# A linear-attention and expert-routing kernel: routing maximum, states' terms, first weights and last outputs rearranged

## The chip, the cores and the metric

The kernel runs on one core of one Trainium2 chip. The metric is the device time of one execution in microseconds (us), as the median of several runs. One execution was also taken by the hardware profiler, which records every instruction of the engines: PE (TensorE matmul; its weight loads are listed as PEld), DVE (VectorE), ACT (ScalarE), POOL (GpSimd) and SP (SyncE, which here only issues transfers).

## The reference

Two blocks follow one another. The first is a linear attention with a decaying state, for 4 batches, 8 heads, 768 steps and 48 elements a head. The second sends each token to one of 8 experts; a local gate decides whether a token takes its own choice or that of the token before it.

```python
for t in range(S):                                   # attention, per batch and head
    cur = einsum('bhd,bhe->bhde', u[None] * kt, vt)
    y[:, :, t] = einsum('bhd,bhde->bhe', rt, state + cur)
    state = w[None, :, :, None] * state + einsum('bhd,bhe->bhde', kt, vt)

logits = einsum('bsd,de->bse', x, w_gate)            # experts; x is y with heads joined, D = 384
local_gate = 1 / (1 + exp(-einsum('bsd,de->bse', x, w_local)))
for b, s:
    fresh_e = argmax(logits[b, s])
    e = fresh_e if s == 0 or local_gate[b, s] < 0.5 else prev_e
    p = softmax(logits[b, s])
    out[b, s] = p[e] * (maximum(x[b, s] @ w1[e], 0) @ w2[e])      # F = 1024
```

## The kernel before

The attention works on 16 items, one for each batch and pair of heads (`M = 16`; item n is batch n // 4, pair n % 4). Sequences are cut into 6 chunks of 128 steps. `Attention.run` is a loop over steps n = 0 to 16 whose order of calls is the order in which each engine gets its instructions; nothing is reordered afterwards. In a step, PE works for item n - 1 and prepares item n + 1:

- `load(n)` issues an item's transfers on SP's queue (`rk`, `kv`, `vT`), three items ahead.
- `scale(n)` on POOL makes `rw` (L229), `ke` (L212) and `pd` (L216), two instructions each. `keys(n)` on DVE makes `kw` (L236) with a factor that lies in PSUM.
- `added(n)` (L248) forms on PE the terms that the chunks add to the state, in the tile `T`, and `states(n)` (L254) runs the decay over them with a DVE scan. `T` is a slice of the one-bank PSUM tile `mp`, which the router also uses.
- `scores(n, g)` (L283) forms the scores within chunks on PE in one of the two `pairs` of PSUM banks, taken in turn by `banks`. The mask is applied on DVE (`am`, L285).
- `own(n)` starts the output `y` on PE (L264), and DVE multiplies it by the values (L268). `inside(n)` (L292) adds the scores' part. `before(n)` (L305) adds the state's part and copies `y` to `xT` (L309, on ACT; for the last item one head on ACT and one on DVE).
- `turn(n)` (L318) transposes an item's outputs to token order in a pair of banks, ACT copies them to `x` (L320), and after a batch's last item they go to DRAM (L323). `logits(b)` (L331) and `token_logits(b)` (L337, L338) compute a batch's routing logits.

Waits follow the tiles: an engine that writes a PSUM bank waits for those that still read that bank of the same tile.

The router works in groups of two batches. For the first group its work is spread over steps 9 to 16 (`g = 8` in `run`): `experts_of` in step 9 (maximum L672, comparison L673, product L674, then L676 to L678 at the end of the step), `keys` (L685) and `runs` in step 10, `turn_runs` (L695), `last` (L702) and `one_hot` (L709 to L713) in step 11, `counts` (L722, L723) and `ranks` (L729 to L738) in step 12, `slots` (L774 to L777) and `columns` (L782) in step 13, `numbers` (L787) in step 14, `places` (L793, `ohq`) in steps 13 and 14, `summed` (L800), `copied` (L806) and `head` (L810 to L831) in step 15. `head` yields the token numbers with which POOL gathers the first expert's rows (L1047, into `xg`).

`Experts` follows: two first units whose experts are fixed, then eight blocks. `fetch` issues a unit's two weight matrices (1.5 MB each). Unit 0's are issued on SP in step 14 of the loop, behind the item loads; SP itself waits for nothing else there, so that they go out at 83.4 and 84.1 us, in step 12 of PE's time. `hidden` (L1074) and `output` (L1161) are an expert's two products; the rows are transposed first (L1060). PE's order at the border is: last `inside` and `before`, the last batch's `logits`, the transposes of the gathered rows, `token_logits`, `hidden`. The PSUM banks of the attention's pools are handed on to the experts' pools in the order in which they lie.

Of the kernel before, what the change touches and what calls it, by code (L numbers as in the profile page):

```python
# [11 lines left out]
F32 = mybir.dt.float32  # L12
# [49 lines left out]
class Attention:  # L62
# [13 lines left out]
    def __init__(self, tc, st, rk_d, kv_d, vT_d, x_d, w_t, wp_d, kept, ident, lt, mp):  # L76
# [13 lines left out]
        self.two = pool("two", 2)  # L90
        self.four = pool("four", 4)
        ps = pool("ps", 1, space=PSUM)

        self.pairs = [ps.tile([P, 2, 512], F32, name=f"pair{i}") for i in range(2)]
        self.py = pool("py", 1, space=PSUM)

# [160 lines left out]
    def own(self, n):  # L257

        nc, t = self.nc, self.items[n]
        t["y"] = y = self.py.tile([P, 2, 512], F32, name="y")  # L260
        for p in range(2):
            for h in range(2):
                q = slice(h * DP, h * DP + DH)
                nc.tensor.matmul(y[p * DP:(p + 1) * DP, h, :C2 * P].rearrange("p (c t) -> p c t", c=C2),  # L264
                                 lhsT=self.w_t[q, t["hp"], 1:2].to_broadcast([DH, DP]),
                                 rhs=t["pd"][q].rearrange("p (c k) t -> p k c t", k=2)[:, p],
                                 start=True, stop=True)
        nc.vector.tensor_mul(y[:, :, :C2 * P], y[:, :, :C2 * P], t["vT"].rearrange("p h c t -> p h (c t)"))  # L268

# [17 lines left out]
    def inside(self, n):  # L287
        nc, t = self.nc, self.items[n]
        for c2, h in [(c2, h) for c2 in range(C2) for h in range(2)]:
            for p in range(2):  # L290
                c = 2 * c2 + p
                nc.tensor.matmul(t["y"][p * DP:(p + 1) * DP, h, c2 * P:(c2 + 1) * P],  # L292
                                 lhsT=t["v"][:, (2 * c + h) * DH:(2 * c + h) * DH + DP],
                                 rhs=t["am"][:, c // 3, h, c % 3], start=False, stop=False, skip_group_check=True)

    def before(self, n):
        nc, t = self.nc, self.items[n]
        if t["hp"] == 0:
            self.xTs[t["b"]] = self.late.tile([P, H, C2 * P], F32, name="xT")
            self.xs[t["b"]] = self.late.tile([P, NCH, D], F32, name="x", bufs=2)  # L300
        for c in range(1, NCH):
            p, c2 = c % 2, c // 2
            for h in range(2):
                q = slice(h * DP, h * DP + DH)
                nc.tensor.matmul(t["y"][p * DP:p * DP + DH, h, c2 * P:(c2 + 1) * P],  # L305
                                 lhsT=t["S"][q, :, c - 1], rhs=t["rw"][q, c],
                                 start=False, stop=True, skip_group_check=True)
        for h in range(2) if n == B * HP - 1 else (slice(0, 2),):
            (nc.vector.tensor_copy if h == 1 else nc.scalar.copy)(  # L309
                self.xTs[t["b"]][:, 2 * t["hp"]:2 * t["hp"] + 2][:, h], t["y"][:, h, :C2 * P])  # L310

    def turn(self, n, banks):

        nc, b, h0 = self.nc, self.items[n]["b"], 2 * self.items[n]["hp"]
        xT, x = self.xTs[b], self.xs[b]
        for h in range(2):
            for c2 in range(C2):
                nc.tensor.transpose(banks[h][:, c2 * P:c2 * P + U], xT[:U, h0 + h, c2 * P:(c2 + 1) * P], self.ident[:U, :U])  # L318
        for h in range(2):
            nc.scalar.copy(x[:, :, (h0 + h) * DH:(h0 + h + 1) * DH],  # L320
                           banks[h][:, :C2 * P].rearrange("p (c e) -> p c e", e=DP)[..., :DH])
        if h0 == H - 2:
            nc.scalar.dma_start(out=self.x_d[b * S:(b + 1) * S, :].rearrange("(c p) d -> p c d", p=P), in_=x)  # L323

    def logits(self, b, bank):

        nc, xT = self.nc, self.xTs[b]
        self.lTs[b] = lT = self.late.tile([P, C2 * P], F32, name="lT")
        for h in range(H):
            j = h % 4  # L330
            nc.tensor.matmul(bank[32 * j:32 * j + 32, :C2 * P], lhsT=self.wp[:, h], rhs=xT[:, h], start=(h < 4), stop=(h >= 4))  # L331
        nc.scalar.copy(lT, bank[:, :C2 * P])
# [8 lines left out]
    def run(self, router, fetch, heads):  # L341
# [11 lines left out]
        for n in range(M + 1):  # L353
            if n + AHEAD - 1 < M:
                self.load(n + AHEAD - 1)
            elif n + 2 == M:
                fetch()
            if n == 0:
# [32 lines left out]
            if n < M:  # L391
                self.turn(n - 2, pair("tp"))
                if n == 3:
                    self.reciprocals(3)
                if n < 5:
                    self.keys(n)
                if n > 3:
                    if n != g + 3:
                        self.added(n)
                    self.states(n)  # L400
# [6 lines left out]
            if n == g + 5:  # L407
                router.slots(0)
                router.columns(0)
            if n == g + 6:  # L410
                router.numbers(0)
            if n == M:
                router.shares(0)
            if n + 1 < M:
                self.scale(n + 1)
            if 3 <= n < 6:
                router.constants(n - 3)
            if n == M:
                self.turn(M - 2, pair("tp"))
            self.inside(n - 1)  # L420
            if n == g + 3:

                router.turn_runs(0, mp[:, mp_end:])
            self.before(n - 1)
            if n == 6:
                router.cast()
# [5 lines left out]
            if n == g + 7:  # L432

                router.summed(0, 0)
                router.copied(0, self.nc.vector.tensor_copy)
                router.head(pair("tb")[0])
                heads()
# [8 lines left out]
            if n % HP == 0:  # L446
# [4 lines left out]
                if n == 4:  # L451
                    self.scores(5, 0)()
                    self.scores(5, 1)()
                    self.keys(6)
                if n == g + 4:
                    router.counts(0, [mp, mp[:, E * NC // 2:]])
                    router.ranks(0, (0,))
# [104 lines left out]
class Router:  # L562
# [103 lines left out]
    def experts_of(self, i, parts=(0, 1)):  # L666
# [3 lines left out]
        if 0 in parts:  # L670
            nc.vector.memset(lt[:, g["z"]].rearrange("p (b c) e -> p b c e", c=NCH)[0:1, :, 0, E:], -1.0)
            nc.vector.tensor_reduce(g["mx"], lg, axis=AX.X, op=Alu.max)  # L672
            nc.vector.tensor_tensor(g["eq"], lg, spread(g["mx"], 2, E), op=Alu.is_equal)  # L673
            nc.vector.tensor_tensor(g["eq"], g["eq"], spread(self.down, 1, g["nc"]), op=Alu.mult)  # L674
# [108 lines left out]

    def numbers(self, i):

        g = self.g[i]
        self.nc.vector.tensor_tensor(g["val"], g["eqv"], spread(self.t1[:, g["z"]], 2, E * ST), op=Alu.mult)  # L787

# [186 lines left out]
class Experts:  # L975
# [49 lines left out]
    def fetch(self, i, engine):  # L1025
# [9 lines left out]
        u["w2"] = wp.tile([P, FK, D], F32, name="w2t", tag="w2t")  # L1035
        engine.dma_start(out=u["w2"].rearrange("p m f -> p (m f)"), in_=w2)

    def gather(self, i, tiles=None, after=None):
# [534 lines left out]
def kernel(  # L1573
# [41 lines left out]
    with ExitStack() as st, tc.manual_schedule():  # L1615
# [4 lines left out]
        att = Attention(tc, st, rk_d, kv_d, vT_d, x_d, w_t, wp_d, kept, ident, lt, router.mp)  # L1620
        att.run(router, lambda: ex.fetch(0, nc.sync), lambda: ex.gather(0))
        ex.open(st)
# [93 lines left out]
```

## Time and profile before

| what | us |
|---|---|
| median of 3 runs (range) | 383.04 (382.22 to 383.92) |
| the profiled execution's own time | 383.35 |
| its span, first to last instruction | 381.6 |
| PE busy | 366.2 |
| DVE busy | 251.4 |
| POOL busy | 150.7 |
| ACT busy | 107.2 |

Steps of the attention loop, by the start of their transposes (L318): step 9 at 62.97 us, 10 at 69.63, 11 at 75.56, 12 at 81.84, 13 at 89.03, 14 at 96.20, 15 at 101.88, 16 at 107.69. The experts' first product (L1074) starts at 114.67.

A line of the timeline gives the start, the length, the engine, the line of the code, the operation, output and inputs by tile name, their shapes, a count of merged instructions, and in brackets the engine's idle time before it with what ended that time. Matmul ends are modelled, so that a busy PE is not PE at its peak; a releaser is inferred, and of several awaited semaphores it is the one that came last. Fp32 products show as two PE instructions each.

### The profile page before, as it was taken

Reading aid. Unit: us, or ns where it says so; the run is one execution under the profiler, and the core shown is the slowest. Engines: PE = TensorE matmul, PEld = TensorE weight load, DVE = VectorE, ACT = ScalarE, POOL = GpSimd, SP = SyncE. Lnnn points to the kernel's source line nnn. Section 1 sums busy time; section 2 is a strip of 40 time slices with the busy share of each in tenths; the row PEclk is TensorE's granted clock in tenths of the full one; section 3 lists DMA queues with packets and bytes.
Section 4 is the critical chain, followed back from the end, with each engine's and each line's share of the span. In section 5 each row is a group of like instructions: output and inputs, shape, how many; then the busy total and the mean of one; then the engine's idle time right before and its main releaser. Section 6 shows DMA issues by size and latency. Waiting matters only on the chain. (4 is left out here: it accounts for less than half of the span.)

```text
span 381.6 us, 9675 instructions
## 1 busy us (share of the span) xinstructions
PE 366.2 (96%) x3846; PEld 322.8 (85%) x3846; DVE 251.4 (66%) x720; ACT 107.2 (28%) x290; POOL 150.7 (39%) x212
## 2 busy tenths in 40 slices
PE   7999999998999999999999999999999999999992
PEld 6776777776759998999999999999998899899971
DVE  6888778978934646596557857758758758466400
ACT  4132232232222211322323233243234233232210
POOL 8689999887222043311422313222323123012022
PEclk9999999999999999999999999999999999999997
DMA  7999999989116881820661254145246156064011
GB/s 252 410 411 408 408 401 326 364 308 381 60 33 226 315 344 37 315 94 23 215 207 55 53 207 189 49 173 214 69 166 227 39 179 228 12 219 165 3 37 36
DMA packets 17477, 74.97 MB, mean 196 GB/s; under 512 B 2729, under 2 KB 6586, under 8 KB 14864
## 3 DMA queue, kind: packets, MB, share of 16 engines
q1 hardware_dynamic: 10048, 56.89, 39.8%
q0 software_dynamic: 3424, 9.52, 7.6%
q10 hardware_dynamic: 3952, 7.87, 5.7%
q8 instruction: 32, 0.52, 0.5%
q14 instruction: 21, 0.17, 0.1%
HBM read 64.83 MB, written 9.51 MB: 195 GB/s over the span
## 5 line engine op out<-in xcount | busy, mean ns | idle before, releaser
L1273 POOL DMA_INDIRECT out_dram<-yo,sid x27 | 26.7, 988 | 102.4 <-ACT yo L1268 75.0
L1124 PE MATMUL h<-exT,w1t 128*128 128x168 f32 (+4 forms) x240 | 54.9, 327 | 0.0
L1128 DVE TENSOR_TENSOR hT<-h,hs 128x168 f32<-128x168 f32 (+3 forms) x60 | 21.1, 351 | 46.5 <-PE h L1124 30.4
L1047 POOL DMA_INDIRECT xg<-x_d,gid x29 | 31.2, 1076 | 37.3 <-DVE sm L882 17.4
L1124 PEld LDWEIGHTS h<-exT,w1t 128*128 128x128 f32 x240 | 41.6, 190 | 0.3 <-issue 0.3
L1074 PE MATMUL h<-exT,w1t 128*128 128x192 f32 (+1 forms) x192 | 38.3, 338 | 0.0
L1193 PE MATMUL y<-factors,sums 128*128 128x192 f32 x168 | 36.8, 326 | 0.0
L1124 PE MATMUL h<-xs,ws 128*128 128x168 f32 (+4 forms) x144 | 35.2, 326 | 0.0
L216 POOL TENSOR_TENSOR pd<-rk 128x384 f32<-128x384 f32 x32 | 31.4, 1002 | 8.6 <-PE y L264 6.2
L285 DVE TENSOR_TENSOR am<-pair,kept 128x768 f32<-128x768 f32 x32 | 30.0, 952 | 6.2 <-PE pair L283 5.5
L1074 PEld LDWEIGHTS h<-exT,w1t 128*128 128x128 f32 x192 | 32.3, 190 | 1.5 <-issue 0.2
L1124 PEld LDWEIGHTS h<-xs,ws 128*128 128x128 f32 x144 | 25.5, 190 | 4.3 <-ACT hs L1131 1.2
L1193 PEld LDWEIGHTS y<-factors,sums 128*128 128x128 f32 x168 | 28.9, 190 | 0.0
L292 PE MATMUL y<-am,kv 128*64 128x128 f32 x384 | 25.4, 276 | 1.2 <-DVE y L268 1.2
L212 POOL TENSOR_TENSOR ke<-kv,endT 128x288 f32<-128x288 f32 x32 | 24.9, 798 | 2.5 <-DMA kv<-in_kv_dram 1.8
L229 POOL TENSOR_TENSOR rw<-rk,tab 128x384 f32<-128x384 f32 x26 | 23.6, 928 | 1.1 <-DMA rk<-in_rk_dram 1.1
L292 PEld LDWEIGHTS y<-am,kv 128*64 128x64 f32 x384 | 21.3, 137 | 3.0 <-DVE y L268 1.7
L309 ACT COPY xT<-y 128x768 f32<-128x768 f32 (+1 forms) x16 | 12.5, 781 | 40.1 <-PE y L305 40.1
L283 PE MATMUL pair<-rw,kw 48*64 48x128 f32 (+1 forms) x768 | 22.8, 249 | 0.8 <-ACT end L167 0.6
L1193 PE MATMUL y<-w2t,hT 128*128 128x192 f32 x96 | 23.0, 328 | 0.0
L1061 DVE COPY exT<-tp 128x384 f32<-128x384 f32 (+6 forms) x29 | 14.0, 490 | 12.8 <-PE tp L1060 12.6
L283 PEld LDWEIGHTS pair<-rw,kw 48*64 48x64 f32 x768 | 19.3, 133 | 2.9 <-ACT end L166 0.8
(279 smaller groups left out, 733.4 us busy)
## 6 DMA issues: line engine op xcount, KB each, us to landing
w1t<-in_w_dram SPq DMA_DIRECT2D x9, 1536.0 KB, 6.7
w2t<-in_w_dram SPq DMA_DIRECT2D x9, 1536.0 KB, 7.3
rk<-in_rk_dram SPq DMA_DIRECT2D x15, 768.0 KB, 9.8
kv<-in_kv_dram SPq DMA_DIRECT2D x16, 584.0 KB, 9.2
vT<-in_vT_dram SPq DMA_DIRECT2D x16, 384.0 KB, 7.4
x_d<-x ACTq DMA_DIRECT2D x4, 1152.0 KB, 9.9
w1t<-in_w_dram ACTq DMA_DIRECT2D x1, 1536.0 KB, 11.2
w2t<-in_w_dram ACTq DMA_DIRECT2D x1, 1536.0 KB, 14.3
```

The source lines that it names most:

```text
L212: nc.gpsimd.tensor_mul(t["ke"][:, p::2], t["k"][:, p::2], spread(self.endT[:, p, hp], 1, C2))
L216: nc.gpsimd.tensor_mul(t["pd"][:, z], t["rT"][:, z], t["kT"][:, z])
L229: engine.tensor_mul(t["rw"][:, z], t["rT"][:, z], spread(pw, 1, z.stop - z.start))
L283: nc.tensor.matmul(sc[f * DP:(f + 1) * DP, h, i, x:], lhsT=t["kw"][q, c, o * DP:(o + 1) * DP], rhs=t["rw"][q, c, x:], start=True, stop=True)
L285: return lambda: nc.vector.tensor_mul(t["am"][:, g], sc, spread(self.kept[:, g:g + 3], 1, 2))
L292: nc.tensor.matmul(t["y"][p * DP:(p + 1) * DP, h, c2 * P:(c2 + 1) * P], lhsT=t["v"][:, (2 * c + h) * DH:(2 * c + h) * DH + DP], rhs=t["am" ...
L1047: self.nc.gpsimd.indirect_dma_start(out=xg[:n], out_offset=None, in_=self.x_d[:rows], in_offset=bass.IndirectOffsetOnAxis(ap=u["gid"][:n, ...
L1074: nc.tensor.matmul(h[:, :n], lhsT=u["w1"][:, m, kk, :], rhs=u["xT"][:, kk, :], start=(kk == 0), stop=(kk == DK - 1))
L1124: nc.tensor.matmul(out, lhsT=a, rhs=b, start=start and k == 0, stop=stop and k == len(terms) - 1, skip_group_check=True)
L1128: nc.vector.tensor_tensor(out, a, b, op=Alu.add)
L1193: return lambda: nc.tensor.matmul(bank[:, x * half:(x + 1) * half], lhsT=a, rhs=b, start=(j == 0 and x == 0), stop=(j == FK // 2 - 1), ski ...
L1273: self.nc.gpsimd.indirect_dma_start(out=out.rearrange("n (h d) -> (n h) d", h=2) if half else out, out_offset=bass.IndirectOffsetOnAxis(ap ...
```

## The change

It has five parts, all in the attention's second half and at the border to the experts.

1. For the first group the maximum of the logits goes to the first 12 columns of `mp` in PSUM, the comparison reads it there, and ACT copies it to `mx` in SBUF for later use.
2. `added(13)` moves from step 13 to step 12, in front of the router's `counts`.
3. Unit 0's weights are fetched in four halves of a matrix (`piece`), in steps 14 and 15. Before each transfer ACT copies one element into the part's place, and the transfer waits for that copy; so ACT's position in the order decides when a part goes out.
4. The last item's `y` lies in one bank of each of the two `pairs`, one for each head, and is multiplied by the values in two instructions. In `inside` and `before` the head becomes the outer loop for that item. Head 0 is copied by ACT to `xT`, head 1 by DVE to a tile of its own, `end7`, which `turn` and `logits` read. The tile `py`, free then, serves `head` and the second-last `turn` as `spare`; the pool `py` is opened before the pairs, so that the banks that the experts' first tiles get are its own.
5. `numbers` of the first group runs on POOL, behind `scale(15)`, instead of on DVE.

```diff
     def own(self, n):
-        t["y"] = y = self.py.tile([P, 2, 512], F32, name="y")
+        last = n == B * HP - 1
+        y = None if last else self.py.tile([P, 2, 512], F32, name="y")
+        t["yy"] = y
+        t["y"] = [self.banks("yl")[:, 0] if last else y[:, h] for h in range(2)]
...
-        nc.vector.tensor_mul(y[:, :, :C2 * P], y[:, :, :C2 * P], t["vT"].rearrange("p h c t -> p h (c t)"))
+        vT = t["vT"].rearrange("p h c t -> p h (c t)")
+        for y, v in [(t["y"][h][:, :C2 * P], vT[:, h]) for h in range(2)] if last else [(y[:, :, :C2 * P], vT)]:
+            nc.vector.tensor_mul(y, y, v)
...
     def before(self, n):
-        for c in range(1, NCH):
+        last = n == B * HP - 1
+        for c, h in [(c, h) for h in range(2) for c in range(1, NCH)] if last else [(c, h) for c in range(1, NCH) for h in range(2)]:
...
+        if last:
+            self.end7 = self.late.tile([P, C2 * P], F32, name="end7")
+            nc.scalar.copy(self.xTs[t["b"]][:, H - 2], t["y"][0][:, :C2 * P])
+            nc.vector.tensor_copy(self.end7, t["y"][1][:, :C2 * P])
...
     def run(self, router, fetch, heads):
-            elif n + 2 == M:
-                fetch()
...
                 self.turn(n - 2, pair("tp"))
+                if n >= M - 2:
+                    fetch(2 * (n - M + 2))
...
-                    if n != g + 3:
+                    if n not in (g + 3, g + 5):
                         self.added(n)
...
-            if n == g + 6:
-                router.numbers(0)
             if n == M:
                 router.shares(0)
             if n + 1 < M:
                 self.scale(n + 1)
+            if n == g + 6:
+                router.numbers(0, self.nc.gpsimd)
...
             if n == M:
-                self.turn(M - 2, pair("tp"))
+                self.turn(M - 2, [self.spare[:, 0], self.spare[:, 1]])
             self.inside(n - 1)
...
             self.before(n - 1)
+            if M - 2 <= n < M:
+                fetch(2 * (n - M + 2) + 1)
...
-                router.head(pair("tb")[0])
+                self.spare = self.py.tile([P, 2, 512], F32, name="y")
+                router.head(self.spare[:, 0])
                 heads()
...
                 if n == g + 4:
+                    self.added(n + 1)
                     router.counts(0, [mp, mp[:, E * NC // 2:]])
...
     def experts_of(self, i, parts=(0, 1)):
-            nc.vector.tensor_reduce(g["mx"], lg, axis=AX.X, op=Alu.max)
-            nc.vector.tensor_tensor(g["eq"], lg, spread(g["mx"], 2, E), op=Alu.is_equal)
+            mx = self.mp[:, :g["nc"]] if i == 0 else g["mx"]
+            nc.vector.tensor_reduce(mx, lg, axis=AX.X, op=Alu.max)
+            nc.vector.tensor_tensor(g["eq"], lg, spread(mx, 2, E), op=Alu.is_equal)
+            if i == 0:
+                nc.scalar.copy(g["mx"], mx)
             nc.vector.tensor_tensor(g["eq"], g["eq"], spread(self.down, 1, g["nc"]), op=Alu.mult)
...
+    def piece(self, k):
+        nc, u, wp = self.nc, self.units[0], self.wps[0]
+        if k == 0:
+            u["w1"] = wp.tile([P, FK, DK, P], F32, name="w1t", tag="w1t")
+            u["w2"] = wp.tile([P, FK, D], F32, name="w2t", tag="w2t")
+        w, z = k // 2, slice(k % 2 * FK // 2, (k % 2 + 1) * FK // 2)
+        t = u["w2"] if w else u["w1"].rearrange("p m k f -> p m (k f)")
+        src = (self.w2 if w else self.w1)[u["e"]].rearrange("p (m x) -> p m x", m=FK)
+        nc.scalar.copy(t[0:1, z.start, 0:1], self.ident[0:1, 0:1])
+        nc.sync.dma_start(out=t[:, z], in_=src[:, z])
```

## The prediction

> **What bounds the kernel now.** I read the page's busy shares first, then the windows, then the timeline of TensorE for gaps, and last DVE and POOL around each gap.
>
> ```profile
> PE 366.2 (96%) x3846; PEld 322.8 (85%) x3846; DVE 251.4 (66%) x720; ACT 107.2 (28%) x290; POOL 150.7 (39%) x212
> 64.00:70.00 6.00, 5.27 (x123) 4.08 (x119) 5.49 (x8) 1.30 (x3) 5.22 (x7) 1.00 0.98 316
> 88.00:94.00 6.00, 4.71 (x77) 3.62 (x73) 4.86 (x11) 1.42 (x4) 4.68 (x6) 1.00 0.98 389
> 160.00:200.00 40.00, 40.00 (x242) 36.87 (x241) 27.20 (x98) 11.23 (x31) 10.09 (x13) 1.00 0.42 149
> ```
>
> Columns of a window: its length, busy PE, PEld, DVE, ACT, POOL, clock, DMA share, GB/s. The experts (from 114.7 us) leave PE no gap until the tail, so what the attention part saves reaches the end whole. What can be saved is PE's idle time before; from step 8 on it is six gaps:
>
> ```profile
> 69.63 0.79 PE L318 MATMUL pair<-ident,xT 112*128 112x112 f32 x6 [0.73 <-DVE am L285]
> 78.67 0.23 PE L695 MATMUL mp<-ident,run 12*128 12x12 f32 x1 [0.91 <-DVE inc L708]
> 91.07 0.66 PE L248 MATMUL mp<-kv,ke 128*48 128x48 f32 x20 [1.29 <-DVE pos L732]
> 101.88 0.80 PE L318 MATMUL pair<-ident,xT 112*128 112x112 f32 x6 [0.33 <-DVE am L285]
> 106.62 0.33 PE L810 MATMUL pair<-ident,rows 128*128 128x128 f32 x1 [0.41 <-DVE rows L806]
> 108.90 1.53 PE L292 MATMUL y<-am,kv 128*64 128x128 f32 x24 [0.42 <-DVE y L268]
> ```
>
> Columns: start, length, what, and in brackets the idle time and who ended it. All six end on DVE. The first starts here:
>
> ```profile
> 65.10 1.68 POOL L229 TENSOR_TENSOR rw<-rk,tab 128x384 f32<-128x384 f32 x2
> 65.65 2.75 DVE L673 TENSOR_TENSOR eq<-lt,mx 128x96 f32<-128x96 f32 x1
> 66.75 1.54 POOL L212 TENSOR_TENSOR ke<-kv,endT 128x288 f32<-128x288 f32 x2
> 68.44 0.26 DVE L674 TENSOR_TENSOR eq<-eq,down 128x96 f32<-128x96 f32 x1
> 68.62 0.95 DVE L285 TENSOR_TENSOR am<-pair,kept 128x768 f32<-128x768 f32 x1
> 72.36 0.63 DVE L677 TENSOR_TENSOR k<-t,k 128x12 f32<-128x12 f32 x1
> 89.50 0.95 DVE L730 TENSOR_TENSOR_SCAN exc<-seg,ext 128x104 f32<-128x104 f32 x1 [0.93 <-ACT ext L729]
> ```
>
> L673 takes 2.75 us beside four POOL instructions and ends as the last of them does (68.29); the same form takes 0.26 at 115.3 with POOL idle. The end of attention:
>
> ```profile
> 111.82 0.56 DVE L309 COPY xT<-y 128x384 f32<-128x384 f32 x1 [2.82 <-ACT xT L309]
> 112.43 0.14 PEld L331 LDWEIGHTS y<-xT,wp 128*32 128x32 f32 x2 [0.45 <-DVE xT L309]
> ```
>
> DVE's half of the last copy waits for ACT's half, and the last logits product for DVE.
>
> **The Trainium skill.** "SBUF — State Buffer", § Who interferes with whom: a DVE instruction with two SBUF inputs contends with a GpSimd instruction that reads SBUF, and the loser fully blocks; one with at most one SBUF input does not contend. The trace agrees: am, y and kw, with a PSUM operand, take 0.92 to 0.97 beside a busy POOL. The page says that whoever issues first gets the ports; here L677, L678, L713, L730 and L738 got in at the first border between POOL instructions after they came, L673 missed three. "TensorEngine Tiling (Array Packing)", § Key Properties: different tiles execute in parallel; L305's 20 instructions of 0.27 us in 0.90 us agree.
>
> **The change part by part.** Times are those of the run before.
>
> *Maximum through PSUM.* L673 drops to 0.26 and ends at 65.95. L674 still has two SBUF inputs and inherits the fight; it needs a border by 67.5 (there are two, 66.75 and 67.50). I take that it gets one. Then am can start when its scores exist, about 67.45, and ends at 68.4; PE, done with L264 at 68.90, does not wait: 0.73 gained. For this to last, DVE's queue to the scan before L695 must move too, since it has no idle time from y (69.48) to 78.61, and PE waits 0.91 for it. y starts 0.12 after L264, at 69.02, 0.46 earlier. L677 comes at 71.90, just before the rw border at 71.96: caught, L678 catches the next (72.96) and the scan is 0.7 earlier; missed, nothing of the gain is left at 78.67. In between, the size is 0.70 or about 0, at worst -0.3. I take 0.70. The copy of mx is a small ACT instruction where ACT idles 2.66 us (before 67.17).
>
> *added(13) before counts.* It takes PE out of the 1.29 gap. But DVE has no idle time from L730 (89.50) until am (95.06 to 96.02), and PE's transposes at 96.20 need that am. PE's gap moves there. added costs about 0.5 and its mode changes 0.2, ahead of counts; ACT had 0.2 of slack, so L730 comes at 89.99, 0.2 before the border at 90.17. Caught: DVE's chain is at most 0.19 later, as POOL's ke no longer waits 0.75 for added and now lies beside L737 and L738. Missed: 0.9 later, less 0.5 that L738 no longer waits, so PE loses 0.2. Bounds +0.15 gain to -0.2; I take 0. DVE's next y still comes 0.3 earlier, as own(13) does.
>
> *numbers on POOL.* Takes 0.53 (L787) from DVE's queue just before am at 100.87, so PE's 0.33 gap goes. On POOL a two-input 128x384 takes 1.0 (L216), in idle time behind pd; own(13) being earlier, it ends near 98.0, before ohq at 99.0. If it collided, 0.4 comes back. I take 0.33 (0.1 to 0.33). summed needs it at 105: hidden.
>
> *Weights in four parts.* The transfers land at 92.3 and 97.1 now and are used from 114.7. SP has nothing behind them until the experts. Four tiny ACT copies are hidden in ACT's idle time. Parts go out at about 97.7, 100.8, 103.4 and 106.4; 0.79 MB at 400 GB/s is 2 us, so the last is in by 110.5. It meets the gather (issued 107.87 and 109.45, landed 111.20 and 112.15), whose rows are needed at 112.8 and 113.3 by the end of this sum. Delay up to 1 us is free. No gain either, as no engine waits for a load between 84 and 97. Cost 0; bound -1.0.
>
> *Last outputs in two tiles.* (a) y comes in two multiplications of about 0.54; the first is done at 108.46, PE is free at 108.48: 0.42 gained. (b) before(15) with h outside: four tiles of the array were busy in turn (20 starts in 0.63 us); now two at a time, up to twice as long. Between 0 and 0.55; I take 0.45. Head 0 is copied meanwhile. (c) Both copies run side by side, and the end7 copy ends at 112.0 instead of 112.38; the last products start at 112.04 and 112.37 instead of 112.43 and 112.78. The first expert's transposes then start at 112.79 instead of 113.19: (a) to (c) together 0.40, up to 0.9 if (b) costs nothing; with half of it 0.65. I take 0.47. Banks of py, pairs and spare change owners without a wait: spare is freed by ACT at 106.3, when PE waits for rows anyway.
>
> Sum: 0.70 + 0 + 0.33 + 0 + 0.47 = 1.5 us. The profiled execution took 383.35 (span 381.6 and 1.75 around it), so it would be 381.85; the median of the runs is 383.04, 0.3 lower, so the forecast is **381.5**.
>
> **The rivals.**
> A, as summed: 381.5 (381.0 to 382.0).
> B, DVE is starved again at L674 or misses at L677, so part one gives nothing: 382.2. For it: L673 missed three borders. Against it: five others missed none.
> C, PE keeps its pace in before(15) (0.9) and step 13 gives 0.15: 2.1 gained, 380.9. For it: L305's weight loads run ahead of the products, so the second head may enter early.
> D, slower, by one mechanism: a DVE instruction with two SBUF inputs is starved for as long as POOL's stream lasts, as L673 was, wherever the change puts one. L674 then ends at 68.4 and part one gives nothing. With added(13) out of the way POOL's rw, rw, ke, ke after 89.35 are one unbroken stream to 92.6; L730 ends at 92.7 instead of 90.45, and less 0.5 for L738 the chain is 1.75 late. PE's transposes start at 97.8 instead of 96.2: 1.6 lost, 0.33 and 0.47 gained, 383.8. It decides from the point where L730 misses the border at 91.1. Against it: five of six got in early.
> E, the gather is 2 us late behind the last part of the weights: its second tile comes at 114.2 instead of 113.3, 0.9 of the 1.5 is lost, 382.4.
>
> **How the numbers follow.** A 0.38, B 0.22, C 0.26, D 0.09, E 0.05. Faster by over 0.5% means under 381.1 (half a per cent is about what a measurement of this kernel tells from no change): most of C, a third of A, a little of B: 0.38. Slower by over 0.5%, above 385.0: the tail of D and what I did not see: 0.07. Range 380.3 to 383.2: it cuts half of D and C's best end.
>
> **What would show it.** L673 near 0.26 and L674's length (under 1.8 right, 2.5 is B); the gaps before L318 at step 10 and L695 at step 11; no gap before L248 in step 13 but one of about 1.2 before the next L318, on am; L787 on POOL before ohq; y's halves and no gap before the last L292; the length of the last L305 (1.4 against 0.9); the landing of xg. I am wrong if the gap of step 13 does not come back behind am, or if the experts do not shift one for one.

## The result and the profile after

| | before | after |
|---|---|---|
| median (range), us | 383.41 (382.22 to 387.05) | 382.08 (381.41 to 387.54) |
| ratio of the times, 95% interval | | 0.9964 [0.9942, 0.9986] |

The change gains 1.4 us, by the interval 0.5 to 2.2. The ratio is taken of fast runs alone and leaves out the changed kernel's one slow run, that of 387.54. The first profile of the changed kernel (span 382.2) and that of tiles_order below hold a stretch at half the TensorE clock from 80.5 us on, for 3.4 and for 6.8 us; so a further profile of the changed code is read here, the run `after_again`, with a span of 380.9, and of tiles_order only what comes later. Line numbers are those of each kernel's own code: L318 of before is L329 here, L673 and L674 are L689 and L692, L695 is L713, L787 is L805, L292 is L297, L305 is L310.

TensorE's idle places in it, and two places where a gap has gone, from the timeline of PE (start, length, what, and in brackets the idle time, where there is any, and who ended it):

```profile
69.07 0.80 PE L329 MATMUL pair<-ident,xT 112*128 112x112 f32 x6 [0.19 <-DVE am L290]
...
78.11 0.23 PE L713 MATMUL mp<-ident,run 12*128 12x12 f32 x1 [0.89 <-DVE inc L726]
...
93.40 0.77 PE L288 MATMUL pair<-rw,kw 48*64 48x128 f32 x24 [0.54 <-DVE lt L349]
...
95.56 0.79 PE L329 MATMUL pair<-ident,xT 112*128 112x112 f32 x6 [0.74 <-DVE am L290]
...
100.79 0.79 PE L329 MATMUL pair<-ident,xT 112*128 112x112 f32 x6
...
105.74 0.30 PE L828 MATMUL y<-ident,rows 128*128 128x128 f32 x1 [0.49 <-DVE rows L824]
...
107.52 1.53 PE L297 MATMUL pair<-am,kv 128*64 128x128 f32 x24
```

Of the six gaps before, those of step 14 (0.33) and of the last outputs (0.42) are gone. The 1.29 in front of `added(13)` has become two, 0.54 and 0.74, together as long. The one at step 11 is as it was (0.89 for 0.91), the one in front of `head` (L810, here L828) is a little longer (0.49 for 0.41), and the one at step 10 is still there.

Lengths of stretches follow from the starts of the transposes (L318 and its like) and of the transposes of the gathered rows (L1060 and its like), each from its own profile, in us:

| profile | 9 to 12 | 12 to 14 | 14 to 15 | 15 to 16 | 16 to rows | first expert product at | from there to the end |
|---|---|---|---|---|---|---|---|
| before | 18.87 | 14.36 | 5.68 | 5.81 | 5.50 | 114.67 | 266.98 |
| before_again | 18.54 | 14.35 | 5.68 | 5.80 | 5.51 | 114.47 | 267.73 |
| after_again | 18.33 | 14.28 | 5.23 | 5.99 | 4.81 | 113.06 | 267.87 |
| undo_added | 19.03 | 14.36 | 5.29 | 5.97 | 4.90 | 113.76 | 267.74 |
| undo_numbers | 19.10 | 14.26 | 5.34 | 5.87 | 4.82 | 113.85 | 266.98 |
| undo_parts | 18.88 | 14.27 | 5.24 | 5.99 | 4.81 | 113.72 | 266.98 |
| undo_last | 18.88 | 14.27 | 5.24 | 5.92 | 5.51 | 114.00 | 267.76 |
| product_psum | 18.14 | 14.26 | 5.24 | 5.99 | 4.81 | 112.80 | 267.88 |
| choice_psum | 18.10 | 14.27 | 5.24 | 5.98 | 4.81 | 112.28 | 267.90 |
| kw_first | 19.22 | 14.04 | 5.24 | 5.98 | 4.82 | 113.35 | 267.85 |
| all_psum | 18.10 | 12.86 | 5.27 | 5.97 | 5.06 | 112.05 | 267.70 |
| all_whole | 18.63 | 12.85 | 5.27 | 5.98 | 4.81 | 113.41 | 266.98 |

Two things have to be kept apart from the change. The code up to step 8 is the same, yet step 9 starts between 62.4 and 64.4 us; and the experts take 266.98 or about 267.8 whatever the kernel. The longer ones have a gap of 0.46 to 0.66 us between 140 and 144 us, where TensorE waits for ACT; why some executions have it stays open. So the stretches are compared, and not the spans. Between before_again and after_again they give: 9 to 12 0.21 shorter, 12 to 14 0.07, 14 to 16 0.26, 16 to the rows 0.70; with 0.17 from the time before step 9 that is the 1.41 by which the first expert product starts earlier. The 0.17 lies ahead of the changed code, and the 0.21 is not of the change either, as the next section shows. So 1.03 is left for it.

### The profile page after: what moved, and what is told of

Same layout as the page of the kernel before. It is cut to its first block, busy times and chain, and to the rows that moved or that the text cites. A ratio compares the mean times of both kernels' runs of the same rounds, so it can differ in the third digit from the quotient of the medians.

```text
span 382.2 us, 9693 instructions
## 1 busy us (share of the span) xinstructions
PE 367.5 (96%) x3846; PEld 324.1 (85%) x3846; DVE 250.6 (66%) x720; ACT 107.5 (28%) x295; POOL 151.3 (40%) x213
## 5 line engine op out<-in xcount | busy, mean ns | idle before, releaser
L297 PE MATMUL y<-am,kv 128*64 128x128 f32 x360 | 23.9, 276 | 0.8 <-DVE y L273 0.8
L297 PEld LDWEIGHTS y<-am,kv 128*64 128x64 f32 x360 | 20.0, 137 | 2.4 <-DVE y L273 1.0
L318 ACT COPY xT<-y 128x768 f32<-128x768 f32 x15 | 12.0, 801 | 34.0 <-PE y L310 34.0
```

Of the source, the lines that this page charges most:

```text
L297: nc.tensor.matmul(t["y"][h][p * DP:(p + 1) * DP, c2 * P:(c2 + 1) * P], lhsT=t["v"][:, (2 * c + h) * DH:(2 * c + h) * DH + DP], rhs=t["am" ...
```

## The experiments

### after_again and before_again: the same two kernels

No edit.

> The changed kernel once more, for a profile in which the clock holds at 1.0 through the attention. If the parts are worth what the first profile shows between its stages, the product of the router (eq<-eq,down) takes about 2.7 us again, PE still waits about 0.65 us at step 10 and 1.0 us at step 11, step 13 has gaps of about 0.6 and 0.7 us, and the first expert product starts 0.9 to 1.1 us earlier than in the kernel before (113.6 to 113.8 us). If the maximum's part works in most executions and that profile was an exception, the product takes under 1.8 us and the step 10 gap is gone.

> The kernel before once more, as the base of this group's profiles. If the 0.6 us wait of PE that the second group of profiles shows in the second expert (before a product with hT, on ACT) belongs to the chip and not to the change, it is here too, and from the first expert product to the end it takes 267.9 us instead of 267.0. If the change causes it, the kernel before has none and takes 267.0 us.

Measured: after_again 0.9961 [0.9947, 0.9976] of before; before_again 0.999 [0.9971, 1.0008]. The long experts, with their gap (0.48), are in before_again too, so they are not of the change. What happens to the routing maximum, from the timeline of DVE and POOL of after_again:

```profile
64.84 1.67 POOL L229 TENSOR_TENSOR rw<-rk,tab 128x384 f32<-128x384 f32 x2
...
65.64 0.25 DVE L689 TENSOR_TENSOR eq<-lt,mp 128x96 f32<-128x96 f32 x1
65.93 2.22 DVE L692 TENSOR_TENSOR eq<-eq,down 128x96 f32<-128x96 f32 x1
...
66.48 1.55 POOL L212 TENSOR_TENSOR ke<-kv,endT 128x288 f32<-128x288 f32 x2
68.07 0.94 DVE L290 TENSOR_TENSOR am<-pair,kept 128x768 f32<-128x768 f32 x1
```

The comparison, which reads the maximum from PSUM, takes 0.25. The product behind it has two inputs in SBUF, starts beside one of POOL's `rw`, and ends at 68.15, when the last of POOL's four back-to-back instructions has ended at 68.03. The borders between them at 66.51 and 67.27 let it pass no more than they did the comparison of before. So it was in each of the ten profiles in which an operation with both inputs in SBUF stands here, the comparison of before or the product of the changed code:

```text
profile        what         starts  takes  ends   POOL's stream ends  gap at step 10
before         comparison   65.65   2.75   68.41  68.29               0.73
before_again   comparison   65.80   1.82   67.61  67.50               0
after          product      65.86   2.67   68.53  68.42               0.65
after_again    product      65.93   2.22   68.15  68.03               0.19
kw_first       product      65.55   3.11   68.66  68.55               1.09
undo_added     product      65.72   2.92   68.64  68.52               0.89
undo_last      product      65.68   2.73   68.42  68.30               0.71
undo_numbers   product      65.96   2.53   68.49  68.38               0.51
undo_parts     product      66.04   2.53   68.57  68.45               0.51
tiles_order    product      65.84   2.66   68.50  68.38               0.64
```

(For kw_first the stream is taken up to its last `ke`, after which `pd` follows.) So the first part of the change put the loss on the next instruction. How large the gap at step 10 is depends on where POOL's stream happens to end, in both kernels; the 0.21 between the two profiles is no gain of the change. The table of stretches bears this out. Take the gap at step 10 from 9 to 12, and the excess of a longer step 10 product where there is one (before_again 0.44, undo_numbers 0.47, all_whole 0.53, see all_whole): 18.10 to 18.17 is left in every profile of it but undo_parts (18.37), in both kernels and in those that follow. The first part of the change was not undone alone.

### product_psum: the comparison's result in PSUM as well

```diff
-            nc.vector.tensor_tensor(g["eq"], lg, spread(mx, 2, E), op=Alu.is_equal)
+            eq = self.mp[:, 16:16 + E * g["nc"]].rearrange("p (c e) -> p c e", e=E) if i == 0 else g["eq"]
+            nc.vector.tensor_tensor(eq, lg, spread(mx, 2, E), op=Alu.is_equal)
...
-            nc.vector.tensor_tensor(g["eq"], g["eq"], spread(self.down, 1, g["nc"]), op=Alu.mult)
+            nc.vector.tensor_tensor(g["eq"], eq, spread(self.down, 1, g["nc"]), op=Alu.mult)
```

> The comparison writes its result to PSUM too, so that the product behind it has one SBUF input. Theory (the product inherited the starving): it takes about 0.26 us, am follows when its scores are there, the gap of 0.65 us at step 10 goes; of that, 0 to 0.7 us is left at step 11, since the next two small instructions (k, key) still have two SBUF inputs. Rival (the stall isn't one of the second SBUF input, or PE waits there for something else as well): the product still takes 1 us or more, or the gap at step 10 stays above 0.4 us.

Measured: 0.9956 [0.9941, 0.997]. The same stretch of its timeline:

```profile
65.46 1.67 POOL L229 TENSOR_TENSOR rw<-rk,tab 128x384 f32<-128x384 f32 x2
65.58 0.26 DVE L690 TENSOR_TENSOR mp<-lt,mp 128x96 f32<-128x96 f32 x1
...
66.13 0.26 DVE L693 TENSOR_TENSOR eq<-mp,down 128x96 f32<-128x96 f32 x1 [0.29 <-ACT mx L692]
67.10 1.55 POOL L212 TENSOR_TENSOR ke<-kv,endT 128x288 f32<-128x288 f32 x2
67.54 0.96 DVE L290 TENSOR_TENSOR am<-pair,kept 128x768 f32<-128x768 f32 x1 [1.15 <-PE pair L288]
...
68.75 0.79 PE L329 MATMUL pair<-ident,xT 112*128 112x112 f32 x6
```

With one input in PSUM the product takes 0.26 in the middle of the same stream, `am` waits for its scores and no longer for DVE, and TensorE has no gap at step 10. That held in all four kernels with this edit. Step 9 to 12 is 18.14, 0.73 shorter than in before's profile, so the gain also survives step 11. before_again, whose comparison happened to end early, has no gap there either; without the 0.44 that its step 10 product is longer (see all_whole) its stretch would be 18.10 too. What the edit takes away is the chance of the loss. Against the changed kernel in the same comparison (382.84 to 383.09) the intervals of the ratios overlap: the stretch shows the effect, the time alone does not.

### choice_psum: the rest of the choice too, all in step 9

On top of product_psum, the next reduction and difference go to PSUM and all of `experts_of` runs in step 9.

```diff
-                router.experts_of(0, (0,))
+                router.experts_of(0)
...
+            k = self.mp[:, 128:128 + g["nc"]] if i == 0 else g["k"]
-            nc.vector.tensor_reduce(g["k"], g["eq"], axis=AX.X, op=Alu.max)
-            nc.vector.tensor_tensor(g["k"], self.t8[:, g["z"]], g["k"], op=Alu.subtract)
+            nc.vector.tensor_reduce(k, g["eq"], axis=AX.X, op=Alu.max)
+            nc.vector.tensor_tensor(k, self.t8[:, g["z"]], k, op=Alu.subtract)
```

> As product_psum, and k and key pass through PSUM and follow at once in step 9, so that none of the five has two SBUF inputs and step 10's queue of DVE is 1.7 us shorter. Theory (DVE's queue from step 9 to the scan in step 11 sets PE's two gaps): no gap at step 10 and one of about 0.65 us at step 11, where PE comes itself 0.65 us earlier; the transposes of step 12 start 0.9 to 1.0 us earlier than in the changed kernel. Rival (PE's gap at step 11 has another cause than DVE's queue): the scores of step 12 start no more than 0.3 us earlier.

Measured: 0.9955 [0.9939, 0.9971]. The three short operations no longer stand between `am` and the scan before step 11's transposes, but the gap there is 0.90, against 0.93 in product_psum, and 9 to 12 is 18.10 against 18.14. TensorE waits there for DVE's row of `y`, `run`, `kw`, `am`, `S`, and in step 10 DVE idles before `y` for TensorE's own product (0.44), which swallows what the shorter choice saved. The expected shortening of the step 11 gap did not come.

### undo_added: added(13) back in step 13

```diff
-                    if n not in (g + 3, g + 5):
+                    if n != g + 3:
...
-                    self.added(n + 1)
                     router.counts(0, [mp, mp[:, E * NC // 2:]])
```

> The changed kernel with added(13) back in step 13. Theory (the gap only moved, DVE's queue decides): a gap of about 1.3 us before added(13) comes back, those of 0.5 and 0.7 us in step 13 go, and from the transposes of step 12 to those of step 14 it takes 14.2 to 14.5 us, as in both kernels (14.36 and 14.28). Rival (the move gained its 1.3 us and another part gave it back): 15.2 us or more.

Measured: one run, 383.2, against 384.37 for before. TensorE's timeline has the old gap again, and the two of 0.54 and 0.74 are gone:

```profile
91.00 0.66 PE L248 MATMUL mp<-kv,ke 128*48 128x48 f32 x20 [1.31 <-DVE pos L749]
```

12 to 14 takes 14.36 with the old order and 14.28 with the new. The ends of DVE's row, from the scan of `ranks` to the `am` on which TensorE's transposes wait, in undo_added and then in after_again:

```profile
89.43 0.96 DVE L747 TENSOR_TENSOR_SCAN exc<-seg,ext 128x104 f32<-128x104 f32 x1 [0.93 <-ACT ext L746]
...
94.99 0.96 DVE L290 TENSOR_TENSOR am<-pair,kept 128x768 f32<-128x768 f32 x1
```

```profile
89.53 0.38 DVE L748 TENSOR_TENSOR_SCAN exc<-seg,ext 128x104 f32<-128x104 f32 x1 [1.52 <-ACT ext L747]
...
94.55 0.95 DVE L290 TENSOR_TENSOR am<-pair,kept 128x768 f32<-128x768 f32 x1
```

With `added(13)` ahead of `counts` the scan starts 8.25 after step 12's transposes instead of 7.66, and the row from there to the end of `am` is 5.97 long instead of 6.52, above all because the scan is shorter. The two nearly cancel: `am` ends 14.22 after step 12's transposes with the new order and 14.18 with the old. Moving the instructions out of the wait left the wait.

### kw_first: DVE's kw of item 14 ahead of counts

```diff
+                if n > 4:
+                    self.keys(n + 2)
                 if n == g + 4:
                     self.added(n + 1)
...
-                if n > 4:
-                    self.keys(n + 2)
```

> The changed kernel with kw of item 14 in front of the router's counts in step 12, where DVE waits for them. Theory (PE's gap of the kernel before has moved behind DVE's queue of step 12 and 13): DVE's am in step 14 comes 0.8 us earlier, the gaps of step 13 (0.6 before the second scores, 0.7 before the transposes) shrink to 0.5 us or less in sum, and everything behind is 0.8 us earlier. Rival (those gaps are due to banks or to POOL): the gaps stay within 0.2 us of their sum of 1.36 us.

Measured: 0.9951 [0.9934, 0.9968], but 12 to 14 only 0.24 shorter (14.04), and the two gaps of step 13 1.05 in sum for 1.28: neither the 0.5 of the theory nor the rival's unchanged sum. Of DVE's chain between the scan and `am`, `kw` (0.94) is taken out; the timelines of POOL and DVE show what came in its place:

```profile
91.04 1.55 POOL L212 TENSOR_TENSOR ke<-kv,endT 128x288 f32<-128x288 f32 x2
```

```profile
90.82 0.30 DVE L754 TENSOR_SCALAR far<-pos 128x24 f32<-128x24 f32 x1
91.15 0.72 DVE L755 TENSOR_TENSOR pos<-pos,far 128x24 f32<-128x24 f32 x1
91.91 0.80 DVE L756 TENSOR_TENSOR pos<-pos,oh 128x96 f32<-128x96 f32 x1
```

L755 and L756 each wait for a border of POOL's `ke`; L756 ends 0.12 after the last one. In after_again L756, behind the end of `ke`, took 0.26. The chain's end is again POOL's end, so DVE's own work was not what set it.

### all_psum: choice_psum, kw_first and the ranks' sums in PSUM

```diff
+            rk = g["rk"].rearrange("p (e c) -> p e c", e=E)
+            g["at"] = rk if i == 0 else g["pos"]
+            nc.vector.tensor_tensor(g["at"], g["exc"][:, :, :n], rk, op=Alu.add)
...
+            at = g["at"]
-                nc.vector.tensor_tensor(g["pos"][:, :EARLY], g["pos"][:, :EARLY], g["far"], op=Alu.add)
-            nc.vector.tensor_tensor(g["pos"], g["pos"], g["oh"], op=Alu.mult)
+                nc.vector.tensor_tensor(at[:, :EARLY], at[:, :EARLY], g["far"], op=Alu.add)
+            nc.vector.tensor_tensor(g["pos"], at, g["oh"], op=Alu.mult)
```

> The changed kernel with the whole choice of experts (comparison, product, k, key) through PSUM in step 9, with kw of item 14 in front of counts, and with the ranks' sums kept in PSUM, so that the last two of them have one SBUF input. Theory (DVE's instructions with two SBUF inputs wait for POOL, and that sets PE's gaps of steps 10 to 14): no gap at step 10; from the transposes of step 12 to those of step 14 13.6 us or less instead of 14.28, since the ranks end about 0.7 us earlier than POOL's ke; the first expert product 0.9 to 1.5 us earlier than in the changed kernel on the same chip; about 1 us in all. Rival (POOL doesn't decide, the gaps have another cause): steps 12 to 14 still take 14.0 us or more.

Measured: 0.9939 [0.9921, 0.9957]. DVE's timeline, and then TensorE's:

```profile
90.44 0.18 DVE L757 TENSOR_SCALAR far<-mp 128x24 f32<-128x24 f32 x1
90.66 0.19 DVE L758 TENSOR_TENSOR mp<-mp,far 128x24 f32<-128x24 f32 x1
90.89 0.26 DVE L759 TENSOR_TENSOR pos<-mp,oh 128x96 f32<-128x96 f32 x1
```

```profile
92.29 1.27 PE L288 MATMUL pair<-rw,kw 48*64 48x128 f32 x46
93.45 0.87 PE L267 MATMUL y<-pd,w_t 48*64 48x384 f32 x8
94.28 0.79 PE L329 MATMUL pair<-ident,xT 112*128 112x112 f32 x6
```

The three operations take 0.63 instead of 1.82 in kw_first, TensorE has no gap from step 12 to 14, and the stretch falls from 14.28 to 12.86. choice_psum alone leaves it at 14.27 and kw_first at 14.04, so the rest is of the ranks' sums, with `kw` out of their way: POOL's stream held DVE's row. The sums in PSUM without moving `kw` were not tried.

A new wait shows at the border: the gathered rows come late.

```profile
110.58 0.88 PE L1093 MATMUL tp<-ident,xg 128*128 128x128 f32 x6 [0.18 <-DMA xg<-x_d,gid]
```

### all_whole and undo_parts: unit 0's weights whole and early

```diff
-                if n >= M - 2:
-                    fetch(2 * (n - M + 2))
...
+            if n + 2 == M:
+                fetch()
...
-        att.run(router, ex.piece, lambda: ex.gather(0))
+        att.run(router, lambda: ex.fetch(0, nc.sync), lambda: ex.gather(0))
```

all_whole is all_psum with this edit, undo_parts the changed kernel with it.

> The version with every DVE operation in question on PSUM operands, but unit 0's weights fetched as two whole matrices early in SP's queue, as before. Theory: the only thing the four released parts do is meet the gather of the first expert's rows (4.51 us from the first issue to the last packet in the version with parts, 3.87 to 3.89 where nothing else moves) - the gather falls to 3.9, the wait of 0.18 us before the transposes of the gathered rows goes, and from the transposes of step 16 to those of the rows it is 4.8 to 4.9 instead of 5.06; nothing changes from step 9 to step 16; span 0.2 us shorter. Rival: the early weights take bandwidth from the item loads or hold SP's queue in steps 12 to 14, and a stretch there gets longer than in the version with parts (12.86 from step 12 to 14, 5.27, 5.97).

> The changed kernel with unit 0's weights as two whole matrices early in SP's queue. Theory: nothing on the path, as the weights are used only from 113 us: every stretch within 0.1 us of the changed kernel's, apart from 9 to 12, which varies with POOL's stream; the gather takes 3.9 us from first issue to last packet instead of 4.3. Rival: the parts had taken load from steps 12 to 14, and 12 to 14 gets longer than 14.28 by 0.3 or more.

Measured: all_whole 380.77 against 383.31, 0.9926 [0.991, 0.9942]; undo_parts one run, 382.47, against the same 383.31. The transfers of all_psum and then of all_whole in the 6 us from the gather's first issue, in slices of 0.15 us (a digit is the busy share of the DMA engines in tenths, so that a 0 can hide a few packets):

```profile
DMA  9847997998973994494231952112000000000000
```

```profile
DMA  0003000000000792674004933100000000000000
```

In all_psum the last part of the weights runs until about the 13th slice, and the gather's last packets are, by the same view's row of GB/s, in the 30th (4.5 us); in all_whole nothing else is under way but a fetch of instructions, and it is the 26th (3.9 us). undo_parts has the 26th too and after_again, by its row of GB/s, the 29th. TensorE's wait for the rows is gone and 16 to the rows takes 4.81 as expected:

```profile
111.94 0.88 PE L1091 MATMUL tp<-ident,xg 128*128 128x128 f32 x6
```

In undo_parts no stretch from step 12 to the rows differs by more than 0.02 from the changed kernel's. So the parts cost the gather 0.45 to 0.6 us, which the changed kernel hides, and bring nothing. In all_whole 9 to 12 came out at 18.63 instead of 18.1; 0.53 of that lies inside step 10's own product, where TensorE stood between two of its instructions with nothing to wait for that the profile shows, from the view of waits:

```profile
PEld y L267 <- issue: 0.4, 1, 0.4
```

The same product is 1.32 to 1.35 long instead of 0.88 in before_again and undo_numbers as well, so this is not of the edit.

all_whole is faster than before and, by after_again's interval [0.9947, 0.9976], than the changed kernel (the first measurement's interval meets it at 0.9942; the three ratios come from different comparisons). Its interval and all_psum's overlap.

### undo_numbers: the numbers on DVE again

```diff
+            if n == g + 6:
+                router.numbers(0)
...
-            if n == g + 6:
-                router.numbers(0, self.nc.gpsimd)
```

> The changed kernel with the numbers on DVE again. Theory: the 0.3 us gap before step 15's transposes comes back and 14 to 15 takes 5.65 to 5.75 instead of 5.23; 15 to 16 returns to 5.8 to 5.9. Rival: the shorter step 14 comes from the earlier own(13), and 14 to 15 stays near 5.25.

Measured: one run, 382.53, against 383.31 for before; 14 to 15 takes 5.34, 15 to 16 5.87. The gap did not come back, and the two stretches together are 11.21, as in the changed kernel (11.22). DVE's timeline in before_again, and then in undo_numbers:

```profile
96.20 0.97 DVE L268 TENSOR_TENSOR y<-y,vT 128x768 f32<-128x768 f32 x1 [0.38 <-PE y L264]
...
100.23 0.53 DVE L787 TENSOR_TENSOR val<-eqv,t 128x384 f32<-128x384 f32 x1
100.69 0.95 DVE L285 TENSOR_TENSOR am<-pair,kept 128x768 f32<-128x768 f32 x1
```

```profile
96.21 0.95 DVE L273 TENSOR_TENSOR y<-y,vT 128x768 f32<-128x768 f32 x1
...
100.23 0.53 DVE L805 TENSOR_TENSOR val<-eqv,t 128x384 f32<-128x384 f32 x1
100.68 0.95 DVE L290 TENSOR_TENSOR am<-pair,kept 128x768 f32<-128x768 f32 x1
```

DVE's row is the same, `numbers` included. But TensorE comes later against it: step 14's transposes start at 96.01 in before_again, 0.19 ahead of DVE's `y`, and at 96.35 in undo_numbers, 0.14 behind it. With `added(13)` moved, TensorE's gap sits behind `am` and `own(13)` is done early, so that DVE has no idle time before `y`, and TensorE none before step 15's transposes. The 0.33 of step 14 is removed twice over, by `numbers` leaving DVE (undo_added: 14 to 15 5.29, with DVE idle for 0.37 before `y` again) and by DVE's idle time going (undo_numbers). Either alone is enough. From step 12 to 16 before_again takes 25.83, the changed kernel 25.50, undo_added 25.62 and undo_numbers 25.47: the two parts together are worth 0.33, but undoing one of them gives back 0.12 or nothing. Both undone, with the rest of the change left in, was not tried.

### undo_last: the last outputs as before

The last item's `y` in `py` again, one multiplication, the old orders, both copies to `xT`.

```diff
-        last = n == B * HP - 1
-        y = None if last else self.py.tile([P, 2, 512], F32, name="y")
+        last = False
+        y = None if last else self.py.tile([P, 2, 512], F32, name="y")
```

> The changed kernel with the last item's outputs as before: one tile y in py, one multiplication, heads inside, both copies to xT, banks as before. Theory: from the last batch's second-last transposes (step 16) to the transposes of the gathered rows it takes 5.5 us as before instead of 4.8 us, and the products of before(15) take 0.90 us instead of 1.19. Rival (the 0.7 us comes from the weights' or banks' new places): 5.0 us or less.

Measured: one run, 383.46, against 384.37 for before. From step 16 to the rows 5.51 instead of 4.81, and the 0.42 before the last L292 is back. But 15 to 16 takes 5.92 instead of 5.99, with the gap in front of `head` at 0.41 again: this part, which also moves `head` to another bank, costs 0.07 there. It is worth 0.70 in its own stretch and 0.63 in all.

### tiles_order: the last before(15) in the old order

```diff
-        for c, h in [(c, h) for h in range(2) for c in range(1, NCH)] if last else [(c, h) for c in range(1, NCH) for h in range(2)]:
+        for c, h in [(c, h) for c in range(1, NCH) for h in range(2)]:
```

> The changed kernel with the last state terms issued in the old order (heads in turn, so that four tiles of the array follow one another), the rest of the last outputs unchanged. Theory: the order of the tiles sets the pace - the group takes 0.90 us again instead of 1.19; head 0 is complete later, so that its copy starts about 0.2 us later, and 16 to the rows' transposes is shorter by 0.1 to 0.3 than 4.81. Rival: the group's 1.19 comes from waiting for the second head's product with the values and not from the order - then it stays near 1.2 and the stretch gets longer.

Measured: one run, 385.43 (before: 383.31), with the half clock in it, of which only the last stretch is read. The group in after_again (from its timeline) and then in tiles_order, with the copies behind it:

```profile
108.98 1.20 PE L310 MATMUL pair<-rw,S 48*48 48x128 f32 x20
...
109.95 0.48 ACT L315 COPY xT<-pair 128x384 f32<-128x384 f32 x1 [1.64 <-PE pair L310]
...
110.21 0.56 DVE L316 COPY end<-pair 128x384 f32<-128x384 f32 x1 [2.13 <-PE pair L310]
```

```profile
112.63 0.90 PE L310 MATMUL pair<-rw,S 48*48 48x128 f32 x20
...
115.29 0.75 PE L1090 MATMUL tp<-ident,xg 128*128 128x128 f32 x4 [0.24 <-DMA xg<-x_d,gid]
...
113.56 0.48 ACT L315 COPY xT<-pair 128x384 f32<-128x384 f32 x1 [1.60 <-PE pair L310]
```

The order sets the pace: 0.90 against 1.20. Head 0's copy starts 0.93 after the group's start instead of 0.97, so even the early copy that the new order is for is not later with the old one. The last logits product ends 4.62 after the start of step 16's transposes instead of 4.88. These 0.26 are then lost to the gather, whose rows come 0.24 after TensorE asks for them; 16 to the rows is 4.86. With the weights whole, and the gather 0.45 shorter, it should show; that is an estimate, as the pair was not tried.

## Why the prediction was right, and where it was not

The time was forecast at 381.5 from 383.04, a gain of 1.5; measured are 1.33 between the medians and 1.4 by the ratio. The terms fare worse than the sum:

| term | predicted | shown by the stretches |
|---|---|---|
| maximum through PSUM | 0.70 | no gain |
| `added(13)` (12 to 14) | 0 | 0.07 |
| numbers on POOL (14 to 16) | 0.33 | 0.26, with `added(13)` as a second cause |
| weights in parts | 0 | 0 |
| last outputs (16 to the rows) | 0.47 | 0.70 |
| sum | 1.5 | 1.03 |

That the time came out so close is in part luck. Of the 0.70 that was missing, the last outputs made up 0.23. The measured interval of 0.5 to 2.2 holds the forecast's 1.5, rival B's 0.8 and the 1.03 alike, and 382.08 itself lies nearer to B's 382.2 than to 381.5. Where the rest between 1.03 and the measured 1.4 comes from is not shown; the gap at step 10 and the experts, which both vary from execution to execution, are where to look.

*Maximum through PSUM.* The step that failed is "I take that it gets one": the product, which inherits the fight, got no border in any of the eight profiles that have it. It took 2.22 to 3.11 instead of 0.26. Rival B, starved again at L674, is what happened. "Five others missed none" weighed too much against the one operation that had missed three, which did the same thing at the same place. The rest of the step was right: product_psum, where the product does pass, has no gap at step 10 and keeps the gain through step 11.

*added(13).* Right in size and in place: the gap moved behind `am`. Not foreseen was that it would split: 0.54 of it is at the second half of the scores, which waits for `lt`'s reduction to free the bank, ahead of the 0.74 on `am`. The scan was put back by 0.58, where the text had 0.49, and was caught at its border, as the text hoped. Rival D needed L730 to be starved too; its like, L748, took 0.38 in after_again. D did not happen.

*Numbers.* The size was about right, for the pair with `added(13)`; for this part alone it was not, as undo_numbers loses nothing. The text had noted that `y` comes earlier by `own(13)` and did not draw from it that DVE would gain slack without `numbers` leaving it. The two parts are not additive. A small loss was missed as well: 15 to 16 is 0.18 longer, of which 0.07 belongs to the last outputs.

*Weights.* As predicted: hidden, and the last part meets the gather. It delayed it by 0.45, not by rival E's 2 us.

*Last outputs.* The term mis-sized most is (b). It was taken as 0.45 of a possible 0.55; the group grew by 0.30 only (0.90 to 1.20). With half the cost the text had 0.65; 0.70 was measured, and 0.63 with the loss in step 15.

*The experts.* They were to shift one for one. They do, but for the 0.8 us by which they differ between executions of either kernel, which the text did not know of.

## What to carry to other kernels

When an operation is slow because of what runs beside it, moving one operand of that operation moves the loss to the next operation with the same kind of operands; edit the whole row up to the next wait, and check the row's end against the end of the other engine's stream. Two changes that each remove the same gap are to be priced as one; undo each of them alone, and if neither brings the gap back, each was enough by itself. A transfer that is hidden today should be looked at again whenever the path ahead of it gets shorter: the gather's delay was free in the changed kernel and became a wait of 0.18 us in all_psum.

## What the hardware showed that was not expected

- A DVE operation of 128x96 with both inputs in SBUF took 1.82 to 3.11 us beside POOL's stream of `rw`, `rw`, `ke`, `ke`, missed two or three borders, and ended 0.11 to 0.12 after the stream in ten of ten profiles; with one input in PSUM, 0.26 in four of four. The Trainium skill, "SBUF — State Buffer", § Who interferes with whom, calls the shared ports an exclusive lock and says that issue order decides who blocks; that the first keeps the ports for its whole instruction is said there of DVE's 2-port modes. A block that lasts over several of POOL's instructions, as here, is not in it. Other operations got through at the next border, of the same shape too (L756 in kw_first, 0.80); what tells the two apart stays open.
- Twenty PE instructions on 48x48 tiles, two to a product, took 0.90 when four tiles followed in turn and 1.20 when two did.
